# A chunk's rearranging DMAs moved from the SP queue to the GpSimd queue

## The chip, the cores and the metric

The kernel runs on one core of a Trainium2 chip. The metric is the device time of one execution in microseconds; the median of three timed runs stands for a kernel. One further execution was profiled, and all rows below come from it.

## What is computed

Three stages follow one another, in float32, on 8 x 576 = 4608 tokens of width 512:

```python
x = attention(q, k, v)                 # 8 heads, causal by blocks of 64
x = max(x @ w_in, 0) ** 2 @ w_out      # 512 -> 2048 -> 512
logits = x @ phi                       # 4608 x 32
d = softmax(logits, over tokens); c = softmax(logits, over slots)
slots = d.T @ x                        # 32 x 512
out = c @ experts(slots)               # 8 experts of 1024
```

## The kernel before

The tokens are cut into 12 chunks of 384. A chunk goes through the second stage in 16 steps, the slots: each slot takes one 128-wide block of w_in and w_out. In a slot, 12 matmuls at L813 (`HB<-MX,W` and `HB<-MX,WL`) make the hidden block in the PSUM bank HB, ACT and DVE square it and split it into a high and a low part (L819 to L824), and 9 matmuls at L838 (`O<-W,MG`, `O<-WL,MG`) add its product with w_out to the banks O. The high parts of the weights, W, stay in SBUF. The low parts are read back from DRAM for every slot: L805 issues one 512 KB load per slot into one of three buffers, WL0 to WL2, as soon as L838 of three slots earlier has read the buffer. The attention of later tokens (L438 to L519; its loads are `aR<-in_kq`, L438, and `aR<-in_v`, L439) is fitted between these matmuls.

When a chunk's 16 slots are done, the generator `moe2` takes its output X (three tiles of 128 x 512). For the logits, x must stand with its columns on the partitions. For eight chunks, the third to finish up to the tenth (called chunk 1 to chunk 8 below), this is done without TensorE: DVE transposes 32 x 32 blocks (L883, three instructions) into XB, a part of the tile aF; one DMA (L886, 768 KB) stores XB in the DRAM tile xt_d; and four DMAs (L889, 192 KB each, 32 partitions x 12 x 128 elements) read it back into YA, with the blocks in their places. L889 waits for L886 to land. The logits (L915, 12 matmuls of YA with phi, on the page also as 24 since they are split) wait for all four. They may not be placed before the first L813 matmul of the slot four after the chunk's end. L926 to L973 follow: the two softmaxes and the weighted sum of x.

All DMAs of the kernel are issued by the queue of SP, which does nothing else, in a fixed order; each DMA in it may wait for semaphores, and what stands behind it then waits too. GpSimd runs a handful of instructions at the start (L344 to L414, `ident`) and then nothing.

The order on every engine is made when the program is built: `Program.order` simulates the engines with a cost for each operation and a due time, and always takes the ready operation that is due first. A DMA on SP is counted as 475 ns of the queue, and its landing as 1160 ns, its bytes at 360 per ns, and 900 ns. On the chip each engine follows that order strictly. At the end, L1165 loads the experts' weights into tiles that come free, among them aF.

Of the kernel before, what the change touches and what calls it, by code (L numbers as in the profile page):

```python
# [21 lines left out]
NTT = CH // 128  # L22
# [24 lines left out]
class Program:  # L47
# [50 lines left out]
    def order(self, banks):  # L98
# [16 lines left out]
        def enqueue(o, now):  # L115
            best = None
            for e, cost, fn in o.alts:
                est = 0.0
                for p, full in o.pred.items():
                    q = ops[p]  # L120
                    est = max(est, q.end + (self.LAT[q.eng][e] if full or q.eng != e else 0.0))
                t = max(est, max(free[e], now) + load[e]) + cost
                if e != o.alts[0][0] and now < EARLY:
                    t += PREFER.get(o.cls, 2500)
                if best is None or t < best[0]:
                    best = (t, e, cost, fn, est)
            _, o.eng, o.cost, o.fn, est = best
            load[o.eng] += o.cost
            heapq.heappush(future[o.eng], (est, o.n))
# [16 lines left out]
        def run_pe(t, cost):  # L146

            while cost > 1e-6:
                k = int((t + 0.01) // WIN)
                slow = 1.0 if act.get(k - 1, 0.0) >= BUSY * WIN else 2.0  # L150
                d = min(cost * slow, (k + 1) * WIN - t)
                act[k] = act.get(k, 0.0) + d / slow
                cost -= d / slow
                t += d
            return t

        while True:
            best, be = None, None
            for e in engs:
                if ready[e] or (e == "pe" and any(modes)):  # L160
                    t = free[e]
                elif future[e]:
                    t = max(free[e], future[e][0][0])
                else:
                    continue
                if best is None or t < best:
                    best, be = t, e
            if be is None:
                break
            t = best  # L170
            while future[be] and future[be][0][0] <= t:
                _, n = heapq.heappop(future[be])
                heapq.heappush(modes[ops[n].mode] if be == "pe" else ready[be], (ops[n].due, n))
            if be == "pe":
                def turn(x):
                    i = modes.index(x)
                    return x[0][0] + (0 if i == mode else JOIN if mode and not i else 0.5 if mode else STAY), x[0][1]
                _, n = heapq.heappop(min((x for x in modes if x), key=turn))
            else:
                _, n = heapq.heappop(ready[be])  # L180
            o = ops[n]
            if o.take:
                gs = o.grp if isinstance(o.grp, list) else [o.grp]
                pool = gs[0].pool
                at = bank_at[pool]
                js = sorted(range(len(at)), key=lambda j: at[j])[:len(gs)]
                kept = keep.get(pool)
                if at[js[-1]] == float("inf") or kept not in (None, n) and ops[kept].due < o.due:
                    parked[pool].append(n)
                    if len(gs) > 1 and kept is None:  # L190
                        keep[pool] = n
                    continue
                if at[js[-1]] > t:
                    heapq.heappush(future[be], (at[js[-1]], n))
                    continue
                if kept == n:
                    keep[pool] = None
                for g_, i in zip(gs, js):
                    g_.bank = i
                    at[i] = float("inf")  # L200
            o.start = t
            load[be] -= o.cost
            if be == "sp" and o.cost:
                free[be] = t + 475.0
                dma_free = max(dma_free, t + 1160.0) + o.nbytes / 360.0
                o.end = dma_free + 900.0
            else:
                c = o.cost
                if be == "pe" and o.mode != mode:
                    mode = o.mode  # L210
                    c += INTO if mode else BACK
                o.end = run_pe(t, c) if be == "pe" else t + c
                free[be] = o.end
            out.append(n)
            if o.give:
                back = o.end + self.LAT[o.eng]["pe"]
                bank_at[o.grp.pool][o.grp.bank] = back
                for p in parked[o.grp.pool]:
                    heapq.heappush(future[ops[p].eng], (back, p))
                parked[o.grp.pool] = []  # L220
            for m in o.succ:
                ops[m].nwait -= 1
                if not ops[m].nwait:
                    enqueue(ops[m], t)
# [34 lines left out]
def c_tr(n):  # L259
    return 100 + 1.08 * n  # L260
# [6 lines left out]
def emit(tc, qk, v, vd, kq2, v2, w, phi, w1, w2, jsel, gsel, out):  # L267
    nc = tc.nc
    pe, act, dve, pool, sp = nc.tensor, nc.scalar, nc.vector, nc.gpsimd, nc.sync
    pr = Program()  # L270
# [16 lines left out]
    xt_d = dram.tile([2, NTT, 128, DM], F32, name="xt_d")  # L287
# [41 lines left out]
    for L, pl_, nm in ((L0, cp, "a"), (L1, late, "b")):  # L329
# [3 lines left out]
        o = NV + 512 + 768  # L333
# [50 lines left out]
    def idle(keys):  # L384


        return [x for k in keys for x in list(pr.readers.get(k, ())) + ([pr.last_w[k]] if k in pr.last_w else [])]
# [476 lines left out]
    def moe2(c, m, due):  # L864

        z = m % 2
# [4 lines left out]
        def k2(nm, o=0):  # L871
            return (nm, (z + o) % 2)
# [5 lines left out]
        if blocks:  # L878
            XB = L0.F[:, 2 * PH_:2 * PH_ + NTT * DM].rearrange("p (t n) -> p t n", t=NTT)
            oldF = idle([("a", "PT", x) for x in range(NPT // 64)] + [("a", "V"), ("a", "VD")])  # L880

            for t in range(NTT):
                pr.add(("dve", c_tr(512), lambda t=t: dve.transpose(  # L883
                    XB[:, t].rearrange("p (j k n) -> p j k n", j=4, k=KT), X2[t].rearrange("p (k j n) -> p j k n", k=KT, j=4))),
                    r=[("X2", t)], w=[("a", "XB", t)], due=due, after=oldF)
            pr.add(("sp", 50, lambda: sp.dma_start(xt_d[z].rearrange("t p n -> p t n"), XB)), r=[("a", "XB", t) for t in range(NTT)],  # L886
                   w=[("xd", z)], due=due, nbytes=3 << 18)
            for j in range(4):
                pr.add(("sp", 50, lambda j=j: sp.dma_start(  # L889
                    YA[32 * j:32 * j + 32].rearrange("p (g x) -> p g x", g=4 * NTT),  # L890
                    xt_d[z].rearrange("t (g p) (j x) -> j p (t g) x", g=4, j=4)[j])), r=[("xd", z)],
                    w=[("YA", t) for t in range(NTT)] if j == 0 else [("YAj", j)], due=due, nbytes=3 << 16)
        for t in range(0 if blocks else NTT):
            g = Group("w")
            for k in range(KT):
                pr.add(("pe", c_mm(128), lambda g=g, t=t, k=k: pe.transpose(
                    bank(g)[:, k * 128:(k + 1) * 128], X2[t][:, k * 128:(k + 1) * 128], ident)),
                    r=[("X2", t), "id"], grp=g, take=(k == 0), due=due)
# [25 lines left out]
        else:  # L924
# [8 lines left out]
            r=[k2("nM")], w=[("LE", 0), k2("sE")], grp=g, give=True, due=due)  # L933
        if m == 0:
            pr.add(("dve", 69, lambda: dve.tensor_copy(T("s"), sE)), r=[k2("sE")], w=[k2("s")], due=due)
        else:
# [4 lines left out]
                   r=[k2("s", 1), k2("al"), k2("sE")], w=[k2("s")], due=due)  # L941
        g = Group("w")
        gt = g
        for a in (1, 0):
            pr.add(("pe", c_mm(128), lambda a=a: pe.transpose(
                bank(gt)[:, a * 128:a * 128 + 96], LE[:, a * 128:(a + 1) * 128], ident[0:96, 0:96])),
                r=[("LE", a), "id"], grp=g, take=(a == 1), due=due)

        def tv():
# [6 lines left out]
               r=["cm"], w=[("cc", c), ("YB",)], grp=g, give=True, due=due)  # L956
# [5 lines left out]
               r=["cs"], w=[("cc", c)], due=due)  # L962
# [9 lines left out]
        else:  # L972
            pr.add(("dve", c_tt(512), lambda: dve.scalar_tensor_tensor(acc, acc, T("al"), bank(gs)[0:96], ALU.mult,  # L973
                                                                       ALU.add)),
                   r=[k2("al")], w=["acc"], grp=g, give=True, due=due)
# [66 lines left out]
    for s, (c, ft) in enumerate(slots):  # L1042
# [15 lines left out]
        while nxt < FT and s >= dec_at[nxt]:  # L1058
# [4 lines left out]
            nxt += 1  # L1063
    slot_o(NS - 1, t_at(NS))
    list(moe2(NCH - 1, NCH - 1, 0))


# [127 lines left out]
    z = (NCH - 1) % 2  # L1195
# [9 lines left out]
    def spread():  # L1205
        for t in range(NTT):
# [4 lines left out]
           r=[("M", z)], w=[("wt",)], grp=g0, due=due - 200)  # L1211
    pr.add(("dve", c_ts(64), lambda: dve.tensor_scalar_mul(J, J, wt)), r=[("wt",)], w=["J"], due=due - 200)
    sin = YA[:, 0:256].rearrange("p (k n) -> p k n", k=KT)
    for j in range(2):
        g2 = Group("w")
        for k in (2 * j, 2 * j + 1):
            pr.add(("pe", 220, lambda k=k, g2=g2: pe.matmul(bank(g2)[:, (k % 2) * 64:(k % 2) * 64 + 64],
                                                            acc[:, k * 128:(k + 1) * 128], J, start=True, stop=True)),
                   r=["acc", "J"], grp=g2, take=(k % 2 == 0), due=due)
# [22 lines left out]
    for g in range(2):  # L1242
# [12 lines left out]
        for n in range(2):  # L1255
# [4 lines left out]
                r=[("fac",)], w=[E1k[g][n], hsbk[g], ("hsb", g, n)], due=due)  # L1260
        for n in range(2):
            gr = Group("w")
            for j in range(4):
                pr.add(("pe", c_mm(128), lambda g=g, n=n, j=j, gr=gr: pe.transpose(
                    bank(gr)[:, j * 128:(j + 1) * 128], hsb[g]()[:, (4 * n + j) * 128:(4 * n + j + 1) * 128], ident)),
                    r=[("hsb", g, n), "id"], grp=gr, take=(j == 0), due=due)
# [56 lines left out]
    for q in range(NQ):  # L1323
# [9 lines left out]
               r=cks, w=[("c3", z_)], due=due_c)  # L1333
# [10 lines left out]
    for h, cl in enumerate(HALF):  # L1344
        gc = Group("w")
        for g in range(2):
            pr.add(("pe", 432, lambda g=g, gc=gc, cl=cl: pe.matmul(bank(gc)[0:96, cl], G[:, g], sob[g][:, cl], start=(g == 0),
                                                                   stop=(g == 1))),
                   r=[("sob", 1, h) if g else ("sob", 0), ("G",)], grp=gc, take=(g == 0), due=due + h)
# [131 lines left out]
```

## Time and profile before

| | |
|---|---|
| median of three timed runs | 1209.46 us (1207.76 to 1210.96) |
| profiled execution, its own time | 1214.7 us |
| its span, first to last instruction | 1212.9 us |
| TensorE matmuls busy | 1157.1 us (95%) |
| VectorE busy | 734.6 us (61%) |
| ScalarE busy | 661.5 us (55%) |
| GpSimd busy | 3.0 us (0%), 16 instructions |
| mean granted TensorE clock | 0.985 of full speed |
| DMA | 227.18 MB, mean 187 GB/s |

Busy times overlap, since the engines run beside each other. What the span depends on is the chain of work that ended last. SP's instructions are DMA issues only and are not counted as busy.

### The profile page before, as it was taken

What the parts mean: (1) busy time and instruction counts of PE and PEld (TensorE: products, weight loads), DVE (VectorE), ACT (ScalarE), POOL (GpSimd) and SP (SyncE); (2) the same over time, 40 slices, a digit from 0 to 9 for tenths busy, and PEclk for the clock granted to TensorE, in tenths of its full rate; (3) what the DMA queues carried; (4) which work ended last, traced back from release to release, by engine and by line L of the source; (5) the groups of instructions that cost most, each with busy time, mean ns of one, the idle gap of its engine ahead of it and who ended that gap; (6) DMA issues with size and microseconds to landing.
All of it is one profiled execution on the core that took longest, in us unless ns stands there. A gap on an engine that the chain in (4) does not pass through costs nothing.

```text
span 1212.9 us, 27938 instructions
## 1 busy us (share of the span) xinstructions
PE 1157.1 (95%) x10967; PEld 964.1 (79%) x10967; DVE 734.6 (61%) x2274; ACT 661.5 (55%) x2087; POOL 3.0 (0%) x16
## 2 busy tenths in 40 slices
PE   6887999999999999999999999999999999999994
PEld 5655887878888888888887888888888887988843
DVE  7999899857556556556557566566576552232213
ACT  7787797765555455455555455455564442232234
POOL 0000000000000000000000000000000000000000
PEclk9998999999999999999999999999999998999997
DMA  6598686543445445446445445445445357366898
GB/s 205 177 305 283 200 263 225 196 138 129 141 138 172 141 143 171 145 134 185 137 138 166 144 141 179 131 144 179 144 144 160 119 181 276 122 225 244 314 390 323
DMA packets 94467, 227.18 MB, mean 187 GB/s; under 512 B 14848, under 2 KB 39168, under 8 KB 94336
## 3 DMA queue, kind: packets, MB, share of 16 engines
q1 hardware_dynamic: 94336, 225.40, 55.9%
q8 instruction: 86, 1.41, 0.5%
q14 instruction: 45, 0.37, 0.1%
HBM read 200.47 MB, written 24.90 MB: 186 GB/s over the span
## 4 chain that ended last, share of the span: by engine, by line
PE 80%; DVE 9%; DMA 7%; ACT 2%; issue 1%; SPq 0%; ACTq 0%; DVEq 0%
PE HB L813 30%; PE O L838 30%; PE B L452 6%; PE B L506 5%; DMA WL<-wlo_d 4%; DVE anm L626 1%; DVE aR L569 1%; PE O L1248 1%; PE B L968 1%; DMA aF<-in_qk 1%; PE B L915 1%; DVE X L770 1%; DVE X L768 1%; PE B L1303 1%; PE B L1291 1%
## 5 line engine op out<-in xcount | busy, mean ns | idle before, releaser
L813 PE MATMUL HB<-MX,W 128*128 128x384 f32 x1536 | 439.2, 345 | 4.4 <-ACT R L819 3.1
L838 PE MATMUL O<-W,MG 128*128 128x512 f32 x1152 | 338.3, 398 | 1.1 <-DVE MG L822 1.0
L813 PEld LDWEIGHTS HB<-MX,W 128*128 128x128 f32 x1536 | 283.0, 190 | 23.6 <-issue 7.8
L813 PE MATMUL HB<-MX,WL 128*128 128x384 f32 x768 | 263.3, 343 | 6.6 <-DMA WL<-wlo_d 6.5
L838 PEld LDWEIGHTS O<-W,MG 128*128 128x128 f32 x1152 | 211.6, 188 | 39.6 <-issue 4.2
L468 ACT ACTIVATE aF<-B,aF 128x192 f32<-128x192 f32 (+8 forms) x432 | 167.0, 420 | 79.4 <-DVE aF L463 70.9
L819 ACT ACTIVATE R<-HB 128x384 f32<-128x384 f32 x192 | 94.8, 494 | 197.9 <-PE HB L813 197.9
L461 DVE TENSOR_REDUCE aF<-B 128x1 f32<-128x192 f32 (+8 forms) x432 | 110.7, 316 | 128.0 <-PE B L452 127.6
L838 PE MATMUL O<-WL,MG 128*128 128x512 f32 x576 | 167.2, 395 | 0.0
L813 PEld LDWEIGHTS HB<-MX,WL 128*128 128x128 f32 x768 | 145.7, 190 | 18.6 <-DMA WL<-wlo_d 10.3
L822 DVE CAST MG<-R 128x384 fp32r<-128x384 f32 x144 | 51.4, 357 | 173.9 <-ACT R L820 169.9
L838 PEld LDWEIGHTS O<-WL,MG 128*128 128x128 f32 x576 | 107.9, 188 | 26.5 <-issue 1.8
L824 DVE TENSOR_TENSOR MG<-R,MG 128x384 fp32r<-128x384 f32 x192 | 105.7, 551 | 10.0 <-ACT MG L822 2.0
L468 ACT ACTIVATION_READ_ACCUMULATOR aF<-B,aF 128x1 f32 x432 | 99.5, 232 | 0.0
L498 DVE STREAM_TRANSPOSE aF<-aF 128x384 f32<-128x384 f32 (+8 forms) x216 | 96.5, 486 | 0.4
L820 ACT ACTIVATE R<-R 128x384 f32<-128x384 f32 x163 | 85.9, 527 | 3.6
L452 PE MATMUL B<-aR 64*32 64x192 f32 (+8 forms) x3456 | 74.9, 301 | 0.0
L452 PEld LDWEIGHTS B<-aR 64*32 64x32 f32 x3456 | 54.7, 105 | 16.6 <-issue 7.2
L494 ACT ACTIVATE aF<-aF 128x256 f32<-128x256 f32 (+5 forms) x146 | 56.0, 435 | 20.9 <-DVE aF L488 20.9
L506 PEld LDWEIGHTS B<-aF,aR 64*64 64x64 f32 x1728 | 52.1, 133 | 19.2 <-issue 9.9
L506 PE MATMUL B<-aF,aR 64*64 64x192 f32 (+8 forms) x1728 | 66.9, 302 | 0.0
L519 ACT COPY xr<-B 128x288 f32<-128x288 f32 x48 | 16.8, 404 | 91.7 <-PE B L506 91.7
(258 smaller groups left out, 1165.6 us busy)
## 6 DMA issues: line engine op xcount, KB each, us to landing
WL<-wlo_d SPq DMA_DIRECT2D x187, 512.0 KB, 3.4
aR<-in_kq SPq DMA_DIRECT2D x24, 576.0 KB, 4.0
aR<-in_v SPq DMA_DIRECT2D x24, 576.0 KB, 3.8
Wr<-in_w SPq DMA_DIRECT2D x16, 512.0 KB, 4.7
aF<-in_w SPq DMA_DIRECT2D x13, 512.0 KB, 7.4
xt_d<-aF SPq DMA_DIRECT2D x8, 768.0 KB, 3.8
YA<-xt_d SPq DMA_DIRECT2D x32, 192.0 KB, 4.5
YA<-in_w SPq DMA_DIRECT2D x11, 512.0 KB, 4.3
```

Of the source, the lines that this page charges most:

```text
L452: pe.matmul(bank(gs[h])[32 * g:32 * g + 32, c:c + 32 * i + 32].rearrange("p (b n) -> p b n", n=32), x[:, S + 64 * i + 32 * q_:S + 64 * i + ...
L461: pr.add(("dve", c_tt(n), lambda g=gs[h], n=n, c=c, x=x: dve.reduce_max(St[:, 0, x:x + 1], bank(g)[:, c:c + n], axis=AX.X, negate=True)), ...
L468: pr.add(("act", c_act(n, ext=2), lambda g=gs[h], n=n, c=c, x=x, i=i, h=h: act.activation(P_(i)[:, h], bank(g)[:, c:c + n], AF.Exp, bias=S ...
L494: act.activation(P_(i)[:, h], P_(i)[:, h], AF.Copy, scale=fct[:, x + h:x + h + 1])
L498: pr.add(("dve", c_tr(2 * n), lambda i=i: dve.transpose(P_(i), P_(i))), w=[K("P2", i, h) for h in range(2)])
L506: pe.matmul(bank(gs[q_])[64 * h:64 * h + 64, 32 * k:288].rearrange("p (i n) -> p i n", n=32), v_2()[sl, h, 64 * k:64 * k + 64], L0.F[sl, o ...
L813: pr.add(("pe", c_mm(CH), lambda a=a, b_=b_, sl=sl, n=n: pe.matmul(HB[:, 0:CH], (WL[i] if a == "l" else W[ft])[:, sl], b_, start=(n == 0), ...
L819: pr.add(("act", c_act(CH), lambda: act.activation(r_, HB[:, 0:CH], AF.Relu)), w=["HB", ("r", j)], due=-1)
L820: pr.add([("act", c_act(CH, True), lambda: act.activation(r_, r_, AF.Square)), ("dve", c_tt(CH), lambda: dve.tensor_mul(r_, r_, r_))], w=[ ...
L822: pr.add([("dve", c_cp(CH), lambda: dve.tensor_copy(gh, r_)), ("act", c_act(CH, True), lambda: act.copy(gh, r_))], r=[("r", j)], w=[("gh", ...
L824: pr.add(("dve", c_tt(CH), lambda: dve.tensor_sub(gl, r_, f(gh))), r=[("r", j), ("gh", j)], w=[("gl", j)], due=-1)
L838: pr.add(("pe", c_mm(512), lambda a=a, b_=b_, sl=sl, t=t, p_=p_: pe.matmul(OB[t], a[:, sl], (WL[i] if b_ == "l" else W[ft])[:, 512:1024], ...
```

## The change

The five DMAs of each of the eight chunks (one at L886, four at L889) are given to GpSimd's queue. In the planner, an operation with bytes is now counted as a DMA whatever its queue, so that a DMA on GpSimd has the same costs as one on SP.

```diff
@@ Program.order
-            if be == "sp" and o.cost:
+            if o.nbytes and o.cost:
                 free[be] = t + 475.0
                 dma_free = max(dma_free, t + 1160.0) + o.nbytes / 360.0
                 o.end = dma_free + 900.0
@@ moe2
-            pr.add(("sp", 50, lambda: sp.dma_start(xt_d[z].rearrange("t p n -> p t n"), XB)), r=[("a", "XB", t) for t in range(NTT)],
+            pr.add(("pool", 50, lambda: pool.dma_start(xt_d[z].rearrange("t p n -> p t n"), XB)), r=[("a", "XB", t) for t in range(NTT)],
                    w=[("xd", z)], due=due, nbytes=3 << 18)
             for j in range(4):
-                pr.add(("sp", 50, lambda j=j: sp.dma_start(
+                pr.add(("pool", 50, lambda j=j: pool.dma_start(
                     YA[32 * j:32 * j + 32].rearrange("p (g x) -> p g x", g=4 * NTT),
                     xt_d[z].rearrange("t (g p) (j x) -> j p (t g) x", g=4, j=4)[j])), r=[("xd", z)],
                     w=[("YA", t) for t in range(NTT)] if j == 0 else [("YAj", j)], due=due, nbytes=3 << 16)
```

On SP's queue, at the first of the eight chunks, the rows before were these (WL_85 to WL_87 are the three buffers):

```order
L805 DMA WL_87<-wlo_d 128x1024
L886 DMA xt_d<-aF 128x3x512
L805 DMA WL_85<-wlo_d 128x1024
L889 DMA YA<-xt_d 32x12x128 x4
L805 DMA WL_86<-wlo_d 128x1024
L805 DMA WL_87<-wlo_d 128x1024
```

With the change, the same place holds the weight loads alone:

```order
L805 DMA WL_87<-wlo_d 128x1024
L805 DMA WL_85<-wlo_d 128x1024
L805 DMA WL_86<-wlo_d 128x1024
L805 DMA WL_87<-wlo_d 128x1024
L439 DMA aR_2068<-in_v 128x1152
```

The two kinds of DMA now stand on GpSimd's queue, behind its last instruction of the start-up, chunk after chunk. The order on SP's queue of what is left is otherwise the same, save at the eighth chunk, where two of seven L1165 loads into aF pass in front of one L805.

On TensorE the logits (L915) keep their place in five of the eight chunks. In the fourth, and in the same way in the seventh, this is the piece of the difference:

```order
 L813 MATMUL HB_68<-MX_94,W4_626 128x384
+L813 MATMUL HB_68<-MX_94,WL1_86 128x384
+L813 MATMUL HB_68<-MX_94,W4_626 128x384
 L915 MATMUL B3_72<-YA_93,ph_79 32x128 x12
-L813 MATMUL HB_68<-MX_94,WL1_86 128x384
 L506 MATMUL B0_69<-aF_104,aR2_2068 64x288 x2
```

L915 stands behind two more matmuls of its slot there. In the eighth chunk it moves further; TensorE's rows from the slot's first matmul to the logits are now these (W_84 and WL_86 are the weights of the slot before):

```order
L813 MATMUL HB<-MX,W_626 128x384
L838 MATMUL O_65<-W_84,MG 128x512
L838 MATMUL O_66<-W_84,MG 128x512
L838 MATMUL O_67<-W_84,MG 128x512
L838 MATMUL O_65<-WL_86,MG 128x512
...
L813 MATMUL HB<-MX,WL_87 128x384
L813 MATMUL HB<-MX,W_626 128x384 x2
L813 MATMUL HB<-MX,WL_87 128x384
L915 MATMUL B_69<-YA,ph 32x128 x12
```

Before, L915 stood right behind the first of these rows; nine matmuls of L838 and four of L813 are now ahead of it. VectorE and ScalarE change their order at this place only.

## Rows read from the trace of the kernel before

**Rows 1.** The page's chain of work that ended last, by engine.

```profile
PE 80%; DVE 9%; DMA 7%; ACT 2%; issue 1%; SPq 0%; ACTq 0%; DVEq 0%
```

**Rows 2.** SP queue's waits: line, releaser, us in total, times, longest.

```profile
SPq L886 <- DVE aF L883: 20.8, 7, 3.4
SPq L889 <- DMA xt_d<-aF: 13.8, 7, 3.0
```

**Rows 3.** TensorE's waits for weight loads, 380 to 990 us; the longest, in the timeline.

```profile
PE HB L813 <- DMA WL<-wlo_d: 1.8, 3, 1.2
...
647.27 0.44 PE L813 MATMUL HB<-MX,WL 128*128 128x384 f32 x1 [1.24 <-DMA WL<-wlo_d]
```

**Rows 4.** SP's queue at the first of the eight chunks: start, length, what.

```profile
387.59 0.37 SPq L886 DMA_DIRECT2D xt_d<-aF  x1
...
391.28 2.44 SPq L889 DMA_DIRECT2D YA<-xt_d  x4
```

**Rows 5.** TensorE's timeline at the logits of chunks 1, 2, 3, 4, 7, 8.

```profile
398.09 1.07 PE L915 MATMUL B<-YA,ph 128*32 128x128 f32 x24
...
488.14 1.07 PE L915 MATMUL B<-YA,ph 128*32 128x128 f32 x24
...
578.39 1.07 PE L915 MATMUL B<-YA,ph 128*32 128x128 f32 x24
...
660.27 1.07 PE L915 MATMUL B<-YA,ph 128*32 128x128 f32 x24
...
920.21 1.07 PE L915 MATMUL B<-YA,ph 128*32 128x128 f32 x24
...
1007.37 1.07 PE L915 MATMUL B<-YA,ph 128*32 128x128 f32 x24
```

**Rows 6.** L889 in chunks 1, 2, 3, 4, 7, 8: issue ns, first and last start; landing.

```profile
L889 SPq DMA_DIRECT2D YA<-xt_d x4: 327/462/1046, 391.3 to 392.7; - x4
DMA to landing us min/median/max: 3.9/4.6/5.2
...
L889 SPq DMA_DIRECT2D YA<-xt_d x4: 424/464/469, 478.0 to 479.5; - x4
DMA to landing us min/median/max: 4.7/5.3/6.2
...
L889 SPq DMA_DIRECT2D YA<-xt_d x4: 318/466/470, 564.8 to 566.1; - x4
DMA to landing us min/median/max: 3.1/3.9/4.7
...
L889 SPq DMA_DIRECT2D YA<-xt_d x4: 319/464/470, 652.0 to 653.3; - x4
DMA to landing us min/median/max: 4.1/4.9/5.7
...
L889 SPq DMA_DIRECT2D YA<-xt_d x4: 319/464/470, 913.6 to 914.9; - x4
DMA to landing us min/median/max: 3.3/4.0/4.7
...
L889 SPq DMA_DIRECT2D YA<-xt_d x4: 318/467/469, 1000.6 to 1002.0; - x4
DMA to landing us min/median/max: 3.2/3.8/4.6
```

**Rows 7.** Twelve L813 matmuls in the chain: start, us.

```profile
343.30 2.10 PE HB L813 x12
```

**Rows 8.** GpSimd's longest instruction: shape, count, busy us, mean ns, idle before.

```profile
L344 POOL MEMSET aF<- 128x768 f32 x1 | 0.7, 738 | 0.0
```

**Rows 9.** DVE's casts from 387 to 398 us, by shape.

```profile
L822 DVE CAST MG<-R 128x384 fp32r<-128x384 f32 x2 | 0.7, 360 | 1.3 <-ACT R L820 1.3
```

**Rows 10.** TensorE behind the eighth chunk's logits; a stretch there, 0.58 its granted clock.

```profile
1018.70 0.44 PE L813 MATMUL HB<-MX,WL 128*128 128x384 f32 x1 [2.36 <-DMA WL<-wlo_d]
...
1018.50:1025.30 6.80, 6.02 (x20) 5.51 (x21) 0.92 (x2) 1.02 (x2) 0.00 (x0) 0.58 0.54 222
```

## The prediction

> **What bounds the kernel.** I first read the page's chain of work that ended last. TensorE is 80% of it and DMA 7% [rows 1], so a microsecond in which TensorE stands still is a microsecond of the result. Then the SP queue's own waits. SP waits for DVE's transposes (20.8 us in seven chunks) and for the store to land (13.8 us in seven) [rows 2]. That is time of a queue that computes nothing; what counts is how often a weight load comes late because SP was held. In the stretch of the eight chunks up to the last one's start TensorE waits for WL 1.8 us in three places, one of them 1.2 us long [rows 3]. Last I set, for each of the eight chunks, the place of the logits on TensorE against the landing of the four loads into YA. TensorE works strictly in order, so if YA is late, L915 holds everything behind it.
>
> **What is removed.** SP loses 40 issues and both kinds of wait. This can give back at most the waits for WL. Of the 1.8 us I credit 0.6: the long one ends at 647.27 [rows 3], before that chunk's loads into YA, which start at 652.0 [rows 6]. The other 0.6 us can lie in the sharing of DMA engines as well as in SP, so this term is generous.
>
> **What is moved, and the margin it has.** The chain of a chunk is: transposes, store, wait, four loads, L915. In the first chunk L886 is issued at 387.59 and the first L889 at 391.28, 3.7 us later [rows 4]. The last L889 starts at 392.7, and with the median landing of 4.6 us YA is there at 397.3 [rows 6]; L915 runs at 398.09 [rows 5]. The margin is 0.8 us. In the same way, last start plus median landing against L915: chunk 2, 484.8 against 488.14, 3.3 us; chunk 3, 570.0 against 578.39, 8.4 us; chunk 4, 658.2 against 660.27, 2.1 us; chunk 7, 918.9 against 920.21, 1.3 us; chunk 8, 1005.8 against 1007.37, 1.6 us. Chunk 5 is like chunk 2 (their landings and places agree within 0.2 us), chunk 6 like chunk 3. The new order adds to three of them. Twelve L813 matmuls take 2.10 us [rows 7], 0.175 us each. L915 goes behind two more in chunks 4 and 7 (0.35 us: margins 2.4 and 1.65), and in chunk 8 behind four more and nine L838 of 512 columns (at 512/384 of 0.175 us, 0.233 each): 0.7 + 2.1 = 2.8, margin 4.4.
>
> **What the moved DMAs cost.** The trace has no DMA issued by GpSimd, so I bound by how much later YA lands, the lateness. Below: GpSimd issues as SP does, lateness 0; I see nothing in the change that shortens the transfers themselves, so no gain. Above: the four loads don't overlap, each starts when the one before has landed: 4 x 4.6 = 18.4 us instead of (392.7 - 391.3) + 4.6 = 6.0 [rows 6], lateness 12.4. Between these, I take GpSimd to write a list of pieces itself. A load is 32 x 12 = 384 pieces, each with a source and a destination, 768 entries; the store, 128 x 3 pieces, has as many. The nearest row is GpSimd's own 768 elements per partition, 738 ns [rows 8]. I add 0.74 us to each DMA, estimated from that row: once for the store, four times for the loads, which one queue writes one after the other. Lateness 5 x 0.74 = 3.7 us. This is the term that I know least.
>
> **The stalls and the sum.** Lateness less margin: chunk 1, 2.9; chunks 2 and 5, 0.4 each; chunk 4, 1.3; chunk 7, 2.05; the other three nothing. Together 7.05 us, less 0.6 for the weight loads: +6.4. The profiled execution's own time of 1214.7 becomes 1221.1 us. It lies 5.2 us above the median of the runs shown, so on the median's scale 1209.5 + 6.4 = 1216 us.
>
> GpSimd's queue has nothing else after the start, so behind its waits stands only the next chunk's DMA. At the eighth chunk the fifth L1165 load into aF must wait until the store has read XB; it now waits for GpSimd's store, and the L805 behind these loads with it. Before, the store had landed by 1000.6, when the first L889 started [rows 6]. I count 0.74 us more as nothing, since an L805 that waits for TensorE stands between the aF loads anyway; if that cover is gone, it costs those 0.74 us.
>
> **A rule weighed.** Beside the loads DVE runs two casts L822 of 360 ns in the stretch from 387 to 398 us [rows 9], and otherwise transposes and two-input operations. The Trainium skill (SBUF — State Buffer, section SBUF: two separate sides, "DVE blocks DMA" trap) says that a DMA from the GpSimd queue has its descriptors written by GpSimd's cores, and that these are locked out while DVE runs a copy or cast in a 2-port mode. If both casts held the list for their whole length, lateness would be 3.7 + 0.7 = 4.4, the stalls 3.6 + 1.1 + 1.1 + 2.0 + 2.75 = 10.6, and the time 1209.5 + 10.6 - 0.6 = 1219.5 us. No run here shows it yet; I keep 3.7, since the casts are 7% of that stretch.
>
> **Rivals.**
> *No measurable change.* 0.3% or 3.6 us is about what a measurement of this kernel can tell from no change. If lateness is 1 to 2.9 us, the stalls are 0.2 to 3.9 and the sum lies between -0.4 and +3.3: 1209 to 1213 us. For it: on SP the issue is 0.46 us of a load's 4.6 [rows 6], so most of it is not the issuer's. Against it: four issues in a row on one queue. The Trainium skill (DMA: Bandwidth & Descriptors, Specifications) puts the first byte of a GpSimd DMA at about 1 us and of an SP one at about 0.6; by that alone the lateness would be an estimated 0.8 us for store and loads together and the time 1209 us.
>
> *Faster.* Behind the eighth chunk's logits TensorE waits 2.36 us for a weight load, and then the granted clock is 0.58 for 6.8 us, between its levels of 2.4 and 1.2 GHz [rows 10]: 0.42 x 6.8 = 2.9 us lost. If SP, freed, gets that load in early enough, and YA is no more than about 1 us later, all of it comes back: 0.6 + 2.4 + 2.9 = 5.9, 1203.6 us. For it: two L1165 loads move ahead and YA leaves SP's queue. Against it: all the same megabytes are still to be moved before that load. It decides below a lateness of 1 us.
>
> *Much slower.* If a list takes GpSimd some 1.4 us, lateness is 7: stalls 6.2, 3.7, 3.7, 4.6, 5.35 and 2.6, together 26; and each, being longer than the one at 1018 us, may bring the same drop of the clock, six times 2.9 = 17. 1209.5 + 43 - 0.6 = 1252 us. At the upper bound (12.4) the stalls are 11.6 + 9.1 + 9.1 + 10.0 + 10.75 + 8.0 and twice 4.0 for chunks 3 and 6, 66.6 us, with eight times 2.9 for the clock: near 1299 us. For it: nothing shows how fast GpSimd is; against it: so few pieces.
>
> **How the numbers follow.** My forecast (lateness 3 to 5, its own range 1213 to 1230) has 0.40, much slower 0.20, no measurable change 0.27, faster 0.13. The lowest edge of the forecast, +3.6 us, touches 0.3%, so 0.02 of its 0.40 goes there: faster 0.13, within 0.3% 0.29, slower 0.58. The range runs from 1204 to 1252: it leaves out half of faster and the worst of much slower.
>
> **What would show it.** Right: TensorE waits at L915 for a DMA into YA, longest in chunks 1 and 7, none in 3 and 6; L889 spaced by over 1 us on GpSimd; SP's waits for DVE L883 and for xt_d gone; waits for WL nearly as before. Wrong: L889 as close as on SP and no wait at L915 (then no change), or waits in all chunks and a lower clock behind them (then much slower); or TensorE at 1018 us without its wait (then faster).

## The result and the profile after

The changed kernel takes 1230.56 us, the median of four timed runs (1226.89 to 1230.98, the lowest being the profiled execution); beside it the kernel before takes 1209.55 us (1207.76 to 1210.96). The ratio is 1.0144, 95% interval 1.0116 to 1.0171: slower. It lies in the range of the prediction (1204 to 1252), 0.6 us above the forecast's own (1213 to 1230). The profiled execution took 1226.89 us against 1214.7 before, +12.2. The other 8.8 us of the difference of the medians is where the two profiled executions lie: before's is 5.2 us over its median, after's is 3.7 under.

The page, for the kernel after: span, busy times, the queue that GpSimd's DMAs use (packets, MB, share), the chain by engine, and the two moved kinds of DMA (count, size, median us to landing).

```profile
span 1225.1 us, 27969 instructions
...
PE 1157.8 (95%) x10967; PEld 963.3 (79%) x10967; DVE 734.8 (60%) x2275; ACT 661.5 (54%) x2086; POOL 28.9 (2%) x56
...
q0 software_dynamic: 3712, 12.59, 3.6%
...
PE 76%; DVE 10%; DMA 8%; ACT 3%; issue 1%; POOL 0%; SPq 0%; ACTq 0%; DVEq 0%; POOLq 0%
...
xt_d<-aF POOLq DMA_DIRECT2D x8, 768.0 KB, 5.4
YA<-xt_d POOLq DMA_DIRECT2D x32, 192.0 KB, 5.1
```

GpSimd's 12.59 MB travel in 3712 packets here. On SP's queue the same bytes take 16000 (its queue falls from 94336 packets on the page before to 78336), and on ScalarE's queue, in a run below, 16000 again.

TensorE's work is the same to 0.7 us, but its share of the chain that ended last falls from 80% [rows 1] to 76%. What it waits for shows why. TensorE's waits after (us in total, times, longest):

```profile
PE HB L813 <- DMA WL<-wlo_d: 9.5, 7, 2.8
PE B L915 <- DMA YA<-xt_d: 8.5, 4, 2.9
```

Before, the first of these was the following, and there was none at L915:

```profile
PE HB L813 <- DMA WL<-wlo_d: 6.5, 7, 2.4
```

So 8.5 us of the 12.2 are new waits for YA, 3.0 are longer waits for weights, and 0.7 is left over. TensorE's timeline after shows where (chunks 1, 4, 5, 7 at L915; the weight waits in chunks 3, 6 and behind the eighth):

```profile
400.69 1.07 PE L915 MATMUL B<-YA,ph 128*32 128x128 f32 x24 [2.44 <-DMA YA<-xt_d]
...
581.14 0.44 PE L813 MATMUL HB<-MX,WL 128*128 128x384 f32 x1 [2.25 <-DMA WL<-wlo_d]
...
666.99 1.07 PE L915 MATMUL B<-YA,ph 128*32 128x128 f32 x24 [2.90 <-DMA YA<-xt_d]
...
756.21 1.07 PE L915 MATMUL B<-YA,ph 128*32 128x128 f32 x24 [0.49 <-DMA YA<-xt_d]
...
846.28 0.56 PE L813 MATMUL HB<-MX,WL 128*128 128x384 f32 x1 [1.75 <-DMA WL<-wlo_d]
...
933.41 1.07 PE L915 MATMUL B<-YA,ph 128*32 128x128 f32 x24 [2.64 <-DMA YA<-xt_d]
...
1025.51 0.44 PE L813 MATMUL HB<-MX,WL 128*128 128x384 f32 x1 [2.81 <-DMA WL<-wlo_d]
```

GpSimd's timeline after gives the moved chain itself, chunks 1 to 4, 7 and 8:

```profile
387.58 0.89 POOL L886 DMA_DIRECT2D xt_d<-aF  x1 [383.97 <-DMA WL<-wlo_d]
393.50 2.45 POOL L889 DMA_DIRECT2D YA<-xt_d  x4 [5.03 <-PE O L838]
476.33 0.76 POOL L886 DMA_DIRECT2D xt_d<-aF  x1 [80.37 <-DVE aF L883]
480.65 2.46 POOL L889 DMA_DIRECT2D YA<-xt_d  x4 [3.57 <-PE O L838]
563.46 0.76 POOL L886 DMA_DIRECT2D xt_d<-aF  x1 [80.34 <-DVE aF L883]
570.35 2.45 POOL L889 DMA_DIRECT2D YA<-xt_d  x4 [6.13 <-PE B L506]
653.72 0.76 POOL L886 DMA_DIRECT2D xt_d<-aF  x1 [80.92 <-DVE aF L883]
659.88 2.46 POOL L889 DMA_DIRECT2D YA<-xt_d  x4 [5.40 <-PE O L838]
...
920.40 0.76 POOL L886 DMA_DIRECT2D xt_d<-aF  x1 [81.98 <-DVE aF L883]
926.64 2.45 POOL L889 DMA_DIRECT2D YA<-xt_d  x4 [5.48 <-DMA xt_d<-aF]
1008.42 0.76 POOL L886 DMA_DIRECT2D xt_d<-aF  x1 [79.32 <-DVE aF L883]
1013.70 2.53 POOL L889 DMA_DIRECT2D YA<-xt_d  x4 [4.53 <-issue]
```

From the store to the first load it is 5.92 us in chunk 1 and 4.32 in chunk 2, where before it was 3.7 [rows 4] and 4.5. All L889 rows except the last show four issues within 2.45 us, 0.61 each. (A row names whichever semaphore moved last; the first load starts 0.53 to 0.67 us after the store's landing in all eight chunks.)

The two lines of code after, over all chunks: issue ns (min, median, max) and landing.

```profile
L886 POOL DMA_DIRECT2D xt_d<-aF x8: 758/760/885, 387.6 to 1008.4; - x8
DMA to landing us min/median/max: 3.8/5.4/6.4
...
L889 POOL DMA_DIRECT2D YA<-xt_d x32: 616/616/694, 393.5 to 1015.6; - x32
DMA to landing us min/median/max: 3.4/5.1/10.0
```

By chunk the store lands after 5.2, 3.8, 6.4, 5.6, 3.9, 6.3, 5.7 and 4.8 us. In chunks 2 and 5 it is as quick as on SP: there SP issues no weight load within 2.5 us of it. In chunks 1, 3, 4, 6 and 7 one follows on SP 0.2 to 0.9 us after the store (at 563.64 in chunk 3), and in chunk 8 the nearest are three loads some 3 us ahead of it and one 2.7 us behind.

### The profile page after: what moved, and what is told of

Its sections match the earlier page's. It is cut to its first block, busy times and chain, and to the rows that moved or that the text cites. A ratio compares the mean times of both kernels' runs of the same rounds, so it can differ in the third digit from the quotient of the medians.

```text
span 1225.1 us, 27969 instructions
## 1 busy us (share of the span) xinstructions
PE 1157.8 (95%) x10967; PEld 963.3 (79%) x10967; DVE 734.8 (60%) x2275; ACT 661.5 (54%) x2086; POOL 28.9 (2%) x56
## 3 DMA queue, kind: packets, MB, share of 16 engines
q1 hardware_dynamic: 78336, 212.82, 51.7%
q0 software_dynamic: 3712, 12.59, 3.6%
## 4 chain that ended last, share of the span: by engine, by line
PE 76%; DVE 10%; DMA 8%; ACT 3%; issue 1%; POOL 0%; SPq 0%; ACTq 0%; DVEq 0%; POOLq 0%
PE HB L813 29%; PE O L838 28%; PE B L452 5%; PE B L506 5%; DMA WL<-wlo_d 5%; DVE anm L626 1%; DMA YA<-xt_d 1%; DMA aF<-in_qk 1%; DVE aR L569 1%; PE O L1248 1%; PE B L915 1%; PE B L968 1%; DVE X L768 1%; DVE X L770 1%; PE B L1303 1%
## 5 line engine op out<-in xcount | busy, mean ns | idle before, releaser
L813 PE MATMUL HB<-MX,W 128*128 128x384 f32 x1536 | 438.5, 344 | 4.6 <-ACT R L819 3.3
L838 PE MATMUL O<-W,MG 128*128 128x512 f32 x1152 | 338.1, 398 | 1.1 <-DVE MG L822 1.0
L813 PEld LDWEIGHTS HB<-MX,W 128*128 128x128 f32 x1536 | 282.4, 189 | 23.8 <-issue 8.0
L813 PE MATMUL HB<-MX,WL 128*128 128x384 f32 x768 | 262.7, 342 | 9.8 <-DMA WL<-wlo_d 9.5
L838 PEld LDWEIGHTS O<-W,MG 128*128 128x128 f32 x1152 | 211.4, 188 | 39.7 <-issue 3.4
L838 PE MATMUL O<-WL,MG 128*128 128x512 f32 x576 | 167.2, 395 | 0.0
L813 PEld LDWEIGHTS HB<-MX,WL 128*128 128x128 f32 x768 | 145.3, 189 | 22.1 <-DMA WL<-wlo_d 14.1
L838 PEld LDWEIGHTS O<-WL,MG 128*128 128x128 f32 x576 | 107.9, 188 | 26.5 <-issue 1.8
```

The source lines that it names most:

```text
L813: pr.add(("pe", c_mm(CH), lambda a=a, b_=b_, sl=sl, n=n: pe.matmul(HB[:, 0:CH], (WL[i] if a == "l" else W[ft])[:, sl], b_, start=(n == 0), ...
L838: pr.add(("pe", c_mm(512), lambda a=a, b_=b_, sl=sl, t=t, p_=p_: pe.matmul(OB[t], a[:, sl], (WL[i] if b_ == "l" else W[ft])[:, 512:1024], ...
```

## The experiments

After the result four causes were open for the lateness and its price: GpSimd's slower issuing; the changed order on the engines; the mere use of a second queue; and the moved transfers meeting others on the DMA engines. My theory was the last: on SP one queue kept the store ahead of the next weight load, on GpSimd it no longer does. Every ratio below is against the kernel before, run on the same chip; in brackets its 95% interval.

### The order alone

The changed kernel's order, but all five DMAs are issued by SP.

```diff
-  ("pool", 50, lambda: pool.dma_start(xt_d[z]...
+  ("pool", 50, lambda: sp.dma_start(xt_d[z]...
-  ("pool", 50, lambda j=j: pool.dma_start(
+  ("pool", 50, lambda j=j: sp.dma_start(
```

> The plan of the changed kernel (every engine's order as with GpSimd DMAs), but the five DMAs of each chunk are issued by SP. Theory (the way through GpSimd makes YA late): the loss goes away, the time is within 3 us of before (1207 to 1212), no wait at L915, L886 lands in 3.8 us again. Rival (the new order on TensorE and SP costs it): still over 1222 us, with waits for WL at chunks 3 and 6 of about 2 us.

Measured: 1218.32 us, 1.0047 [1.0022, 1.0071]. TensorE's waits in this run:

```profile
PE HB L813 <- DMA WL<-wlo_d: 4.6, 4, 2.9
PE B L915 <- DMA YA<-xt_d: 3.5, 3, 1.7
```

This lies between the two expectations: the loss does not go away altogether, but most of it does. Run on SP, the new order costs about 0.5%: with the five DMAs planned on a queue of their own, L805 falls between the L889 on SP, and the last part of YA is late in chunks 1, 4 and 7. The other percent goes with GpSimd's queue. How much of the 0.5% is in the changed kernel too isn't shown, since no L805 can stand between the L889 there. There are no weight waits in chunks 3 and 6 here.

### The store alone, and the loads alone

One of the two kinds is issued by GpSimd, the other by SP, in the changed kernel's order.

Store alone on GpSimd:

```diff
-  ("pool", 50, lambda j=j: pool.dma_start(
+  ("pool", 50, lambda j=j: sp.dma_start(
```

Loads alone on GpSimd:

```diff
-  ("pool", 50, lambda: pool.dma_start(xt_d[z]...
+  ("pool", 50, lambda: sp.dma_start(xt_d[z]...
```

> Only the store L886 is issued by GpSimd, the four loads L889 by SP again. Theory: the store lands about 1.6 us later (5.4 instead of 3.8), the loads need 4.5 as before, so TensorE waits at L915 about 1 us in chunk 1 and at most 1 us in 4 and 7; SP stands 1.6 us longer at L889, which delays WL a little: 1211 to 1217. Rival (YA's packets on a second ring slow the weight loads): no waits for WL at chunks 3 and 6, within 3 us of before.

> Only the four loads L889 are issued by GpSimd, the store by SP again. Theory (lateness): the loads start 1.7 us later and the last issue is 0.6 us later, YA about 2 us late, waits at L915 of 1 to 1.5 us in chunks 1, 4 and 7; 1212 to 1218. Rival (second ring): the waits for WL at chunks 3 and 6 (2.2 and 1.8 us) stay, and the time is nearer to the changed kernel's, 1218 to 1226.

Measured: store alone 1229.66 us, 1.0148 [1.0101, 1.0195]; loads alone 1221.78 us, 1.0090 [1.0064, 1.0116]. I had put the store alone at 1211 to 1217, and that failed. The store's waits and landing when it alone is moved: SP's wait for it, then its line.

```profile
SPq L889 <- DMA xt_d<-aF: 30.3, 7, 5.9
...
L886 POOL DMA_DIRECT2D xt_d<-aF x8: 762/762/881, 391.5 to 1015.9; - x8
DMA to landing us min/median/max: 3.8/5.5/7.2
```

SP's waits for the store went from 13.8 us [rows 2] to 30.3, in seven chunks, and the weight loads stand in SP's queue behind them: TensorE waits for WL 11.0 us in ten places, and 6.1 us at L915. The store on GpSimd is thus late whoever issues the loads. When it is on SP and the loads on GpSimd, it lands after 3.4 to 5.4 us, median 3.6, and TensorE's waits at L915 fall to 2.5 us. That run missed too: the time is over the 1212 to 1218 of the theory, but the weight waits in chunks 3 and 6, by which the rival was to be known, are not there.

### All five on ScalarE's queue

```diff
-  ("pool", 50, lambda: pool.dma_start(xt_d[z]...
+  ("act", 50, lambda: act.dma_start(xt_d[z]...
-  ("pool", 50, lambda j=j: pool.dma_start(
+  ("act", 50, lambda j=j: act.dma_start(
```

> All five DMAs of a chunk on ACT's queue: a queue apart from SP's, but without GpSimd. Theory (GpSimd's lateness): store lands in about 3.8 us, YA is on time, no wait over 1 us at L915 and none over 1 us for WL at chunks 3 and 6; within 6 us of before, as with the same plan on SP (1.0047). Rival (any second ring beside SP's slows the weight loads): waits for WL of 2 us at chunks 3 and 6 again, over 1222 us. ACT's own waits at the loads may add up to 1 us per chunk in either.

Measured: 1218.78 us, 1.0057 [1.0036, 1.0078], hardly more than the order alone. The store on ACT's queue:

```profile
L886 ACTq DMA_DIRECT2D xt_d<-aF x8: 383/383/397, 387.4 to 996.8; - x8
DMA to landing us min/median/max: 3.4/3.6/5.2
```

Of the 5.7 us that TensorE waits at L915 here, 4.53 stand in the eighth chunk, where none over 1 us was expected; the time is 8 us over before's 1210.69 on that chip, not within 6. But a second queue is not what makes the store late. Chunk 3 shows it best, since there SP issues a weight load within half a microsecond of the store in each kernel:

| chunk 3 | store issued, landed after | weight load issued, landed after |
|---|---|---|
| before, both on SP | 560.84, 3.9 | 561.31, 4.8 |
| store on ACT | 563.06, 4.2 | 563.51, 5.1 |
| store on GpSimd | 563.46, 6.4 | 563.64, 4.3 |

On ACT the store, issued first, also lands first. On GpSimd it lands 1.9 us after a load that was issued 0.18 us later. The store's lead over the load differs, 0.45 us against 0.18, and the single packets in the traces show what that does. The store's first packet starts 0.90 us after the issue on SP and 0.92 on ACT; on GpSimd it is 1.33 where nothing lies beside it. In chunk 3 the weight load's first packet starts 1.14 us after GpSimd's store is issued, ahead of the store, and the store's first packet then waits until 3.48 us.

### The weight load beside the store taken away

In chunks 1 to 8 the one L805 load that is issued beside the store is left out (the matmuls that follow read what the buffer held).

```diff
-  lambda: sp.dma_start(f(WL[i]), wlo_d[ft])
+  lambda: ft == 3 and 3 <= c <= 10 or sp.dma_start(f(WL[i]), wlo_d[ft])
```

> The changed kernel without the one weight load per chunk (block 3 of the next chunk, eight loads in all) that SP issues while GpSimd's store is under way; that block is then computed with older low parts. Theory as it stands now (alone, GpSimd's store is hardly slower; it is late where the weight load of the other queue gets in beside it): the store lands in 3.7 to 4.1 us in all eight chunks, the waits at L915 fall from 8.5 to under 3 us, 1213 to 1222. Rival (GpSimd's own slowness): landing still 5 us and more, L915's waits over 6 us.

Measured: 1226.18 us, 1.0103 [1.0066, 1.0139]. The store, and L915 in chunks 1 and 8:

```profile
L886 POOL DMA_DIRECT2D xt_d<-aF x8: 758/758/885, 389.0 to 1002.7; - x8
DMA to landing us min/median/max: 3.8/3.8/8.2
...
401.04 1.07 PE L915 MATMUL B<-YA,ph 128*32 128x128 f32 x24 [1.71 <-DMA YA<-xt_d]
...
1025.69 1.93 PE L915 MATMUL B<-YA,ph 128*32 128x128 f32 x24 [8.28 <-DMA YA<-xt_d]
```

In seven chunks the store lands after 3.8 to 4.0 us: without the load beside it, GpSimd's store is on time. The rest of the expectation failed: the waits at L915 are 12.6 us in all, and the time is over 1222. One reason is the eighth chunk, where SP issues one L805 and four L1165 loads, 512 KB each, in the 3.8 us ahead of the store (998.86 to 1002.68; the changed kernel had two L1165 there). The store lands after 8.2 us, and L915 waits 8.28. The other is that in chunks 1, 4 and 7 the store is on time and YA still is not: of 8.0 us of waits at L915 there, 4.3 stay (1.71, 0.47 and 2.10). The late store thus explains about half of them. The loads into YA are slower here, the last one landing after 5.4 to 6.3 us where it took 4.7 to 5.2 in the changed kernel.

### The store in three pieces

```diff
-  pr.add(("pool", 50, lambda: pool.dma_start(xt_d[z].rearrange("t p n -> p t n"), XB)), ...
+  for t in range(NTT):
+      pr.add(("pool", 50, lambda t=t: pool.dma_start(xt_d[z][t], XB[:, t])), ...
```

> The changed kernel with the store L886 split into three DMAs of 256 KB, each issued by GpSimd right behind its own transpose. If what GpSimd pays is by pieces written (my 0.74 us), each issue takes about 0.3 us and the stores land 1 us or more sooner after the last transpose than now (5.4): 1216 to 1224. If it pays a fixed time per DMA, each issue takes 0.6 us or more, and the time stays within 3 us of the changed kernel.

Measured: 1228.58 us, 1.0133 [1.0099, 1.0167], no better than one store. Lines are moved by one here, so the store is L887:

```profile
L887 POOL DMA_DIRECT2D xt_d<-aF x24: 539/557/710, 388.1 to 1010.9; - x24
```

An issue of 256 KB in 128 pieces takes 557 ns, one of 768 KB in 384 pieces 758: a third of the work still costs 73%. By these two, some 0.46 us of an issue (557 - (758 - 557)/2) are fixed, and cutting a DMA up on this queue pays that part again. Pieces and bytes both seem to count in the rest: a load, 384 pieces too but 192 KB, takes 616 ns.

### The logits two slots later, after and before

If TensorE only loses time because YA is late, moving L915 back should bring it back. The same edit in the changed kernel, and in the kernel before as a control:

```diff
-            part = (s + 4, g_)
+            part = (s + 6, g_)
```

> The changed kernel, with the logits placed two slots later (the generator is resumed at slot s + 6 instead of s + 4), some 8 us more margin for YA. Theory: the waits at L915 (8.5 us in four places) vanish; what is left is the waits for WL: 1213 to 1222. If lateness were not the cause (an engine slowed by GpSimd's work, the clock): 1227 or more.

> The kernel before (DMAs on SP) with the logits two slots later, as the run x4_later did with DMAs on GpSimd. If placing the logits later costs nothing by itself, within 4 us of before; then what x4_later still lost (14 us, no wait at L915 in it) is the lateness of GpSimd's DMAs acting on the weight loads. If the later place itself costs (collisions with the v and k, q loads move), over 1220 us.

Measured: changed kernel 1226.15 us, 1.0125 [1.0084, 1.0166]; before 1217.99 us, 1.0060 [1.0040, 1.0080]. The first missed its 1213 to 1222, and the control is 7.3 us over before, neither within 4 nor over 1220. Of the two groups of waits for these DMAs, the changed kernel with later logits has one left:

```profile
PE HB L813 <- DMA WL<-wlo_d: 13.0, 11, 3.2
```

The 8.5 us of waits at L915 are gone, and the waits for weights are 13.0 us (9.5 with the early logits). In the control they rise by as much, from 6.5 to 9.9, so the later place brings some 3.4 us of them on either queue. The control has none in chunks 3 and 6; the changed kernel has, and chunk 3's grows from 2.25 to 3.22. So the later place takes away the price that is paid at L915, and leaves the one that is paid at the weight loads: against its control the changed kernel still loses 0.65% (1.0125 against 1.0060).

### A planner that knows the slower DMA

GpSimd's DMAs are counted as 700 ns of the queue and 3000 ns before the first byte.

```diff
-  free[be] = t + 475.0
-  dma_free = max(dma_free, t + 1160.0) + o.nbytes / 360.0
+  free[be] = t + (475.0 if be == "sp" else 700.0)
+  dma_free = max(dma_free, t + (1160.0 if be == "sp" else 3000.0)) + o.nbytes / 360.0
```

> The changed kernel, but the planner counts a GpSimd DMA with 700 ns of the queue and 3000 ns before its bytes, instead of 475 and 1160, near what the changed kernel's trace showed. Theory: the logits are placed behind YA's landing, waits at L915 fall from 8.5 to under 2 us; waits for WL stay or grow as in x4_later: 1.0 to 1.3% over before. If the plan was all that was wrong: within 0.5% of before.

Measured: 1225.95 us, 1.0110 [1.0084, 1.0135]. As expected, the planner puts the logits later, no wait at L915 is left, and the waits for weights are 10.1 us in seven places (3.21 at 584.67, in chunk 3). Honest costs don't win the percent back.

### A quarter of YA, on GpSimd and on SP

The two kernels with later logits, each with three of the four L889 left out: 24 transfers of 192 KB, 4.7 MB.

```diff
-  lambda j=j: pool.dma_start(
+  lambda j=j: j or pool.dma_start(
```

The second kernel has sp in place of pool in both lines.

> The run x4_later (GpSimd DMAs, logits two slots later), but three of the four loads into YA are left out, so the logits are computed from a YA of which a quarter is new. Theory (YA's late loads run into the v and weight loads of SP): the waits for WL at chunks 3, 5 and 6 of x4_later (3.2, 1.2, 1.9 us) fall below 0.5 us each, the time is within 1215 to 1221. Rival (the store, or GpSimd's queue as such, delays the weight loads): they stay.

> The kernel before with the logits from slot six, as in x5_before_later, and with three of the four loads of every chunk left out, as in x9_quarter: the logits read only a quarter of YA that is new. It is the control of x9_quarter, which went from 1.25% slower to no difference. Theory (GpSimd's later issue costs nothing by itself; it costs because late YA loads lie beside the weight load): without those bytes the queue no longer matters, so this kernel takes the same time as x9_quarter within 0.4%, 1206 to 1215 us where the kernel before takes 1211. Rival (the queue costs something of its own also without the bytes, and x9_quarter only hides that behind what 4.6 MB fewer give back): this kernel is then 5 us or more faster than the kernel before, 1206 us or less.

Measured: on GpSimd 1210.61 us, 0.9985 [0.9965, 1.0006]; on SP 1212.59 us, 0.9990 [0.9969, 1.0010]. On GpSimd the store still lands after 3.8 to 6.4 us, and in chunk 3 the load starts 7.0 us after the store (566.61 and 559.59). But now that costs nothing; in the stretch of the chunks one weight wait of 0.41 us is left, behind the eighth, and none in chunks 3 and 6. I had expected 1215 to 1221, so these bytes were worth more than I thought: 1.4% on GpSimd (1.0125 to 0.9985) and 0.7% on SP (1.0060 to 0.9990). Without them the queue makes no difference that can be told, as the second expectation had it. With the logits this late, GpSimd's lateness is paid for only where the late loads into YA lie on top of the weight loads.

### The changed kernel again

> The changed kernel once more, on the same chip as its neighbours here: 1.2 to 1.7% over before. Its trace shows whether the waits for WL at chunks 3 and 6 (2.25 and 1.75 us) and at L915 (8.5 us in all) repeat, or were one execution's.

Measured: 1234.46 us, 1.0181 [1.0155, 1.0208], a little over the 1.2 to 1.7%; at L915 9.0 us of waits in four, for WL 7.3 in seven, 2.69 of it at 582.59 in chunk 3. The pattern repeats. The profiled execution took 1225.62 us at a mean granted clock of 0.990; the other four 1234.01 to 1234.93 us at 0.977 to 0.983, where the kernel before had 0.985 to 0.991, mean 0.988. The lower clock goes with some 9 us that the profile doesn't show.

## Why the prediction was right, and where its size was off

**TensorE in order, and YA late: right.** The waits stand at L915, in chunks 1, 4 and 7 as the longest (the prediction had named 1 and 7), 0.49 us in chunk 5, none in 3 and 6. SP's waits for DVE L883 and for xt_d are gone. Counting from the store's issue, YA was to be there after 9.7 us in chunk 1 (397.3 - 387.59); L915's wait ended after 13.1 (400.69 - 387.58). That is a lateness of 3.4 us; 3.7 were predicted.

That these two agree is in part luck. The prediction let the last of the four loads land after the median time; the longest landing is the last one's, 5.2 us in chunk 1 [rows 6]. By it YA was there at 397.9 before, the margin was 0.2 us and not 0.8, and the lateness is 2.8 us. A margin and a lateness that were both too large cancel. All the margins shrink by 0.6 to 0.9 us in this way. Nor is the lateness one number: from the store's issue to the last landing YA takes 1.0 us less than before in chunk 2 and 7.4 us more in chunk 3.

**The terms of the stall.** Predicted 2.9, 1.3 and 2.05 us for chunks 1, 4 and 7, 0.4 each for 2 and 5; measured 2.44, 2.90, 2.64, nothing and 0.49. Together 8.5 against 7.05. Chunk 4's is the one that was mis-sized. There the load into YA ended 13.3 us after the store's issue (666.99 - 653.72), where before it was 9.6 by the prediction's own arithmetic (658.2, with the store issued at 648.55): lateness 3.6, near the 3.7 (2.7 by the longest landing). So the margin it was set against was not there: TensorE stood at L915 10.4 us after the store (666.99 - 2.90 - 653.72), where before it was 11.7 (660.27 - 648.55). In chunks 1 and 7 these times agree within 0.2 us of the prediction's. The reason is a weight wait that went away. Before, the 1.24 us that ended at 647.27 [rows 3] lay between the chunk's last L838 (ended at 645.9) and L915. After, the same matmul starts at 650.77, right behind the one ahead of it (650.60). So TensorE comes to L915 1.24 us sooner, but YA does not, and what was won at the weight load is waited for at L915. That is most of the 1.6 us by which chunk 4's stall was too small.

**Why it is late: the sum was near, its parts were others.** The issue on GpSimd costs 0.62 us for a load and 0.76 for the store, near the 0.74 taken from a MEMSET [rows 8]. But that was added in full five times, and SP's issues take 0.46 and 0.37 us [rows 4, 6]: what comes on top is 0.15 to 0.39 each, about 1.0 us over a chunk's five. The L889 stand 0.61 us apart, not "over 1 us". The 3.4 us of chunk 1 are made up otherwise. The store lands 1.6 us later (5.2 against 3.6). From its landing to the first load it is 0.7 us, on SP 0.1. From the first load to the end of L915's wait it is 7.2, against 6.0 in the prediction and 6.6 by the longest landing. In chunk 3 the store alone is 2.5 us later (6.4 against 3.9), in chunk 2 not at all. The prediction treated the transfer itself as unchanged. The runs without the weight load (3.8 us in seven chunks) and on ScalarE's queue (3.6 us) show that GpSimd's transfer loses when it stands beside one of SP's.

**The step that failed: the weight loads.** The prediction gave 0.6 us back on WL, as SP was to be freed. Measured is +3.0 in the profile. The 1.8 us of rows 3 are all gone, more than was credited; but in the same stretch 4.0 new ones stand, 2.25 us in chunk 3 and 1.75 in chunk 6, which had none before and were counted as safe, their margin at L915 being 8.4 us. There is no wait at L915 in them, but in chunk 3 the margin is used up. The rows after, for its loads into YA and its logits:

```profile
L889 POOL DMA_DIRECT2D YA<-xt_d x4: 616/616/632, 570.3 to 572.2; - x4
DMA to landing us min/median/max: 5.3/7.1/8.7
...
583.26 1.07 PE L915 MATMUL B<-YA,ph 128*32 128x128 f32 x24
```

YA is there at 580.9, and without the weight wait L915 would have stood ready at 581.0. What stopped TensorE first is another transfer. The chain of the kernel after in chunk 3, in order of time:

```profile
571.23 0.45 PE O L838
571.68 0.01 issue
571.70 9.40 DMA WL<-wlo_d
581.10 0.04 issue
581.14 2.19 PE HB L813 x11
```

A 512 KB load takes 9.40 us; the one issued in the same place before landed after 5.4. The loads into YA start at 570.35 instead of 564.8 [rows 6]. Of these 5.6 us 2.6 come from the stall of chunk 1 (the store is at 563.46 instead of 560.84), and 3.0 are lateness: they now lie beside aR's load, issued at 570.29, and this WL. With a quarter of YA's bytes this wait is gone, as the run above with later logits shows. In the stretches of the two kernels (length, then busy of PE, PEld, DVE, ACT, POOL, then the granted clock, DMA share, GB/s), first after:

```profile
566.00:572.00 6.00, 6.00 (x116) 4.39 (x115) 2.27 (x9) 1.72 (x4) 1.65 (x3) 1.00 0.61 205
572.00:578.00 6.00, 6.00 (x133) 5.25 (x132) 3.22 (x13) 2.84 (x10) 0.80 (x2) 1.00 0.99 261
578.00:584.00 6.00, 3.75 (x37) 3.03 (x38) 1.70 (x11) 3.42 (x16) 0.00 (x0) 1.00 0.76 222
```

and before:

```profile
566.00:572.00 6.00, 6.00 (x112) 4.87 (x104) 1.78 (x6) 2.02 (x8) 0.00 (x0) 1.00 1.01 254
572.00:578.00 6.00, 6.00 (x133) 5.36 (x133) 3.91 (x18) 3.51 (x16) 0.00 (x0) 1.00 0.55 183
```

The DMA engines' full stretch moved from 566 to 572 us, where no weight was urgent, to 572 to 578, where one was; TensorE then has 3.75 busy us of 6.

**The median's scale.** 6.4 us were added to the median, +21 were measured. Of the 14.6 missed, the profile shows 5.8 (the weights 3.6, the stalls 1.5, unassigned 0.7), and 8.8 lie between the profiled executions and the medians. In the repeat the runs' clocks go with that (0.977 to 0.983 against 0.990), in the measurement itself they hardly do (0.984 against 0.985). The prediction's "much slower" rival had priced such drops, at a lateness of 7. It was wrong in its lateness, but a part of its clock term may be in the time. How much of the 8.8 us is the clock stays open, since an execution that is only timed shows no more than its mean.

**The rivals.** "No change" needed a lateness under 2.9. The page that spoke for it (the Trainium skill, DMA: Bandwidth & Descriptors, Specifications) gave an estimated 1209 us by its first bytes; store and load alone bear its small price out (the store lands after 3.8 us alone on GpSimd, 3.4 to 4.2 on SP in chunks 1 to 7, and its first packet starts 1.33 us after the issue against 0.90), but it has no term for the load beside them. "Faster" fell with the wait behind the eighth chunk, which is 2.81 us at 1025.51 instead of 2.36 [rows 10]. The granted clock behind it is different, though. The stretch of 6.8 us at 0.58 is gone; a shorter one stands behind the wait of chunk 6:

```profile
846.30:849.80 3.50, 3.50 (x11) 3.24 (x11) 0.00 (x0) 0.51 (x4) 0.00 (x0) 0.52 0.33 134
1025.00:1032.00 7.00, 5.99 (x48) 4.05 (x49) 2.94 (x12) 2.23 (x8) 0.00 (x0) 1.00 1.03 414
```

It costs 0.48 x 3.5 = 1.7 us where before 2.9 were lost.

**The rule that was weighed.** The Trainium skill (SBUF — State Buffer, "DVE blocks DMA" trap) was given 0.7 us per chunk at most. The longest issues are 885 ns against a median of 760 for the store and 694 against 616 for a load: at most 0.13 us, and 0.15 with the store in three pieces (710 against 557). No run here shows more of it.

## What to carry to other kernels

A queue is also an order. Before a DMA is moved off a shared queue, look at which transfers stand just behind it there: they will be issued beside it, and the price is paid by whichever of the two TensorE waits for first, which need not be the moved one. Check margins for the neighbours' landings, not only for the consumers of what is moved; and where a later consumer trades one DMA wait for another, as the later logits do in part, the thing to reduce is the bytes in that stretch.

No version tried beats the kernel before: the two that tie with it leave three quarters of YA's loads out.

## What the hardware showed unexpectedly

A 768 KB store issued by GpSimd lands after 3.8 to 3.9 us when SP issues no weight load within 2.5 us, and after 5.2 to 6.4 us when one follows within 0.9 us, even where SP's load is issued 0.18 us later; that load lands after 4.3 us. From ScalarE's queue, in the same place, the store lands after 4.2 us and the weight load after 5.1. The Trainium skill (DMA: Bandwidth & Descriptors, Issuing engines are not separate DMA queues) says that DMAs of all issuing engines run on the same 16 DMA engines and interleave, so that a second issuer saves only issue time. ScalarE's queue agrees with it here; on GpSimd's the store lost up to 2.5 us.

The single packets of the store show that both things happen that can make it late:

| chunks, changed kernel | weight load issued after the store by | store's first packet after | first to last packet |
|---|---|---|---|
| 2, 5 | 2.6 us or more | 1.33 to 1.34 us | 2.0 us |
| 1, 4, 7 | 0.6 to 0.9 us | 1.33 to 1.47 us | 3.3 to 4.0 us |
| 3, 6 | 0.2 us | 3.41 to 3.48 us | 2.5 to 2.6 us |

In chunks 3 and 6 the store begins later, in 1, 4 and 7 it is slowed once it has begun. On SP and on ScalarE's queue its first packet starts after 0.89 to 0.93 us in chunks 1 to 7, and it takes 2.1 to 3.0 us. Why SP's load gets between the packets on GpSimd's queue stays open; that these are fewer and larger than on the other two queues (3712 against 16000) is a difference that no run tried by itself. GpSimd also begins the load that waits for the store 0.5 to 0.7 us after the landing in all eight chunks; in the kernel before, SP began it after 0.3 us at most.
